# Spreading the weight-narrowing steps of the first chunk and moving one w_out product

## The chip, the cores and the metric

The kernel runs on one core of a Trainium2 chip. The metric is the device time of one execution in microseconds (us); less is better. A core has TensorE (PE, matrix products), VectorE (DVE), ScalarE (ACT), GpSimd (POOL) and SyncE (SP), which here issues all transfers. Each engine takes its own instructions in order, and semaphores make it wait for the others.

## The reference

Three stages follow one another, with a batch of 8, 8 heads, 576 positions of 64 values, and 4608 tokens of 512 values in all:

```python
p_packed = sm_attn(p, k, v)               # 32 packed queries per head
x = sm_attn(q, p_packed, p_packed)        # then tokens x 512
xn = x / rms * rms_g
g = xn @ w_gate; val = xn @ w_val         # 512 x 1536
x = (g * sigmoid(g) * val) @ w_out        # 1536 x 512
h = x @ w_in                              # 512 x 2048
out = (max(h, 0) + alpha * min(h, 0)) @ w_out2
```

The weight matrices come as 64-bit floats, the other inputs and the output are 32-bit floats.

## The kernel before, in words

**Chunks and tiles.** The first two stages run together over 12 chunks of tokens (up to 512 each), the third stage follows. This change touches chunk 0 alone (c = 0), which runs with 512 tokens. A chunk passes through 12 tiles f of 128 of the 1536 hidden values. For each tile TensorE computes the gate group and the value group (`blk_in`, L1012, into the PSUM banks g and v), ScalarE the Silu of g (L1071), VectorE the product s with v (L1078). In odd tiles s is then split into a high part hh on ScalarE and a remainder hl on VectorE, with the remainder in_l of the tile's w_out block in between (both L113); in even tiles of chunk 0 it is used as it is. `blk_out(f)` (L1033) multiplies s by the tile's block of w_out into four banks y: on L1037 for even tiles of chunk 0, on L122 to L124 for odd ones. It is called one tile late, as `blk_out(f - 1)`.

**Narrowing.** The weights come as 64-bit words. `narrow` (L224) makes a unit of 128 x 512 weights into 32-bit floats in two halves. Half A is L227 on VectorE and L231 on ScalarE, half B is L233 on VectorE and then L236 on GpSimd, whose result is the finished unit. There are 36 units: for every pair of tiles j, four units of gate and value weights (gv) and two of w_out (o). `conv_all` (L323) is a generator that takes two units at a time and yields after every half, so a pair is four steps: A, A, B, B. With the end of a unit, which it notices at the step after the pair's last B, it counts the unit in `n_conv` and issues further loads on the SP queue (`loads_to`), as far as load buffers are free (8 for the first 18 units, 4 for the others). A narrowed gv unit is also stored to DRAM for the later chunks; the last three are stored only with unit 34. `conv(n)` runs n steps, `conv_to(n)` runs steps until n units are counted.

**Places in a tile.** `work(f, at)` runs at four places of a tile: 1 after the Silu, 2 after s and its splitting, 3 after the first burst, 4 after the second. It lets the attention chains for the next tokens make their VectorE and ScalarE steps and then, in chunk 0, runs narrowing steps: two at each of the places 1, 2 and 3, none at 4. `burst(f, 2)` and `burst(f, 3)` put TensorE work of these chains (transposes, scores: L420, L429, L442, L481, L600, L617) into the queue.

**Jobs.** The gate and value weights are first multiplied by the packed attention output. `wg_job(b, j)` (L725) does this for batch b and pair of tiles j with 16 matmuls on L735, four for each of its four gv units, and splits the two results (wgh, wgl), which `blk_in` of the tiles 2j and 2j+1 reads. In chunk 0, job (0, 0) runs in the prologue, job (0, j+1) at the start of `burst(f, 2)` of tile f = 2j+1, hence in the tiles 1, 3, 5, 7 and 9, and job (1, 0) in tile 11. Job (0, 5) also issues the reloads of stored units for the jobs (1, 0) and (1, 1) into the ring of 8 gv buffers (L722).

**Order.** The kernel schedules by hand: every engine runs its instructions in the order in which the program issues them. At the start of a tile of chunk 0 the kernel before calls

```python
j1 = (f + 1) // 2
conv_to(min(6 * j1 + (5 if f % 2 else 6), NU1))
```

and the order around the job is

```python
burst(f, 2)            # in chunk 0 with the tile's job ahead
work(f, 3)
if 0 < f < NF - 1:
    blk_out(f - 1)
if f < NF - 1:
    burst(f, 3)
```

In `both` (L359), called at the end of the even tiles of chunk 0, the w_out unit of the next tile is split.

Of the kernel before, what the change touches and what calls it, by code (L numbers as in the profile page):

```python
# [18 lines left out]
def attention_moe_moe2_kernel(ctx, tc, q, k, v, p, w_gate, w_val, w_out, rms_g, w_in2, w_out2, alpha, out):  # L19
# [8 lines left out]
    NF = FF // 128  # L28
# [97 lines left out]
    with tc.manual_schedule():  # L126
# [65 lines left out]
        NU1 = len(units)  # L192
# [24 lines left out]
        def new_gv():  # L217
            return one.tile([128, 4, 128], F32, tag="gv", name="gv_raw", bufs=8)
# [19 lines left out]
        def conv_unit(n):  # L238
            if n == NU1 // 2:
                sg_ctx.close()  # L240
                late_pools["wg2"] = ctx.enter_context(tc.tile_pool(name="wg2", bufs=NWG - NWG1, reuse_waits="tile"))
            u = units[n]
            w = new_gv() if u[0] == "gv" else wa.tile([128, 4, 128], F32, tag="w", name="w_raw")
            yield from narrow(staged.pop(n), w)
            raw[u] = w
            if u[0] == "gv":
                stores.append((u[1], w))
            while stores and (len(stores) > 3 or n >= NU1 - 2):
                i, w = stores.pop(0)
                nc.sync.dma_start(out=gv_dram[i], in_=w.rearrange("p c x -> p (c x)"))  # L250
            yield

        def conv_late():
# [55 lines left out]
                products((5, b22), (3, b21))  # L309
            yield  # L310

        n_load, n_conv, n_job = [0], [0], [0]

        def loads_to(n):
            while n_load[0] < min(n, NU1):
# [28 lines left out]
        def conv(n):  # L344
            for _ in range(n):
                next(convs, None)

        def conv_to(n):
            while n_conv[0] < min(n, NU1):
                next(convs)  # L350

        in_s = {}
# [372 lines left out]
        def wg_job(b, j):  # L725
            if b >= B:
                return
            need_k(b)
            n_job[0] += 1
            ts = [bank("wg") for _ in range(G)]  # L730
            us = [raw.pop(("gv", j * 4 + dc)).rearrange("p c x -> p (c x)") for dc in range(HG)]
            for c_ in range(HG):
                for e in range(2):
                    g, h = c_ // 2, c_ % 2 * 2 + (e ^ c_ // 2)
                    nc.tensor.matmul(  # L735
                        out=ts[g][h * NP:(h + 1) * NP, :],
                        lhsT=ppG[b][e * D:(e + 1) * D, c_, :],
                        rhs=us[c_][e * D:(e + 1) * D, :],
                        start=True, stop=True,
                        tile_position=(e * D, h * NP),  # L740
                    )
            for g in range(G):
                pool = wg1 if n_wg[0] % NWG < NWG1 else late_pools["wg2"]
                n_wg[0] += 1
                h_ = pool.tile([128, 512], F32R, tag="wgh", name="wgh")
                l_ = pool.tile([128, 512], F32R, tag="wgl", name="wgl")
                split_hi(h_, ts[g])
                split_lo(l_, ts[g], h_)
                wgt[b, j, g] = (h_, l_)
            m = b * NJ + j  # L750
            for x in (m + 1, m + 2) if m == NJ - 1 else (m + 2,) if m >= NJ else ():
                gv_load(x)
# [184 lines left out]
        for c, (t0, n, cuts) in enumerate(CH):  # L937
# [9 lines left out]
            def work(f, at):  # L947
                live = [ch for ch in chains["k"] if ch.kind is not None][:1] + chains["q"]
                swap = c > 0 or at == 3 and any(ch.kind == X or ch.kind == M for ch in live)
                if swap and c == 0:  # L950
                    preload(ACTF.Exp)
                for ch in live:
                    n_ = 0
                    while n_ < 2:
                        if ch.kind == R and (at == 1 or at > 2 and (ch is first[0] or n_ == 0)):
                            pass
                        elif n_ == 0 and ch.kind == E and (c == 0 or at < 4) or swap and ch.kind == M:
                            pass
                        elif ch.kind == X and swap and (c == 0 or at == 1 and n_ == 0 or f == NF - 1):
                            pass  # L960
                        else:
                            break
                        ch.last = (c, f, at)
                        ch.next()
                        n_ += 1
                if swap and c == 0:
                    preload(ACTF.Silu)
                if c == 0:
                    conv(2 if at < 4 else 0)

            def q_turn(now, free):
                for n_, ch in enumerate(chains["q"]):
# [21 lines left out]
            def burst(f, at):  # L994
                first[0] = None
                if at == 3 and c and any(ch.kind == X for ch in chains["k"]):
                    return
                jobs = JOBS[c].get(f, ()) if at == 2 else ()
                for jb in jobs if c == 0 else ():
                    wg_job(*jb)  # L1000
                now = [(c, f, x) for x in ((1, 2)[c == 0:] if at == 2 else (2, 3) if c else ())]
                free = 0 if jobs and c else 2
                need = any(ch.b not in ppG for ch in chains["q"])
                if need and (at == 2 or f % 2 == 0):
                    q_turn(now, k_turn(now, free))
                else:
                    k_turn(now, q_turn(now, free))
# [25 lines left out]
            def blk_out(f):  # L1033
                if c == 0 and f % 2 == 0:
                    h, w = hs.pop(f), raw["o", f]
                    for d in range(KD):
                        nc.tensor.matmul(out=ybk[d], lhsT=w[:, d, :], rhs=h, start=f == 0, stop=f == NF - 1)  # L1037
                    return
                oh, ol = in_s.pop(("o", f))
                hh, hl = hs.pop(f)  # L1040
                for d in range(KD):
                    mm3(ybk[d], oh[:, d, :], ol[:, d, :], hh, hl, f == 0, f == NF - 1)

            for f in range(NF):
                if c == 0 and f == 1:
                    held, hold[0] = hold[0], None
                    for i in held:
                        load_q(i)
                if c == NP1 - 2 and f == 9:
                    y_rows.append(load_rows(0, 0))  # L1050
                if c == 6 and f == 6:
                    nc.sync.dma_start(out=alpha_sb, in_=alpha.rearrange("(f p) -> p f", p=128))
                if c == 0:
                    j1 = (f + 1) // 2
                    conv_to(min(6 * j1 + (5 if f % 2 else 6), NU1))
                if last:
                    if f == 0:
                        assert next(late, late) is late
                        prepare = prep(0)
                    if f > 0:  # L1060
                        next(prepare, None)
                    if f in (2, 4, 6, 8, 10):
                        next(prepare, None)
                    if f > 2:
                        load_next()
                tg = blk_in(f, 0, "g")
                s = ring.tile([128, T], F32, tag="s", name="s")[:, 0:n]
                if c:
                    nc.scalar.activation(out=s, in_=tg, func=ACTF.Tanh, scale=0.5)  # L1069
                else:  # L1070
                    nc.scalar.activation(out=s, in_=tg, func=ACTF.Silu)  # L1071
                work(f, 1)
                if c:
                    nc.vector.scalar_tensor_tensor(  # L1074
                        out=s, in0=s, scalar=1.0, in1=tg, op0=ALU.add, op1=ALU.mult
                    )
                tv = blk_in(f, 256, "v")
                nc.vector.tensor_tensor(out=s, in0=s, in1=tv, op=ALU.mult)  # L1078
                for jb in JOBS[c].get(f, ()) if c else ():
                    wg_job(*jb)  # L1080
                exact = c == 0 and f % 2 == 0
                hs[f] = s if exact else hsplit(s, n)
                if c and 0 < f < NF - 2:
                    work(f, 2)
                if not exact:
                    split_lo(hs[f][1], s, hs[f][0])
                if not (c and 0 < f < NF - 2):
                    work(f, 2)
                burst(f, 2)
                work(f, 3)  # L1090
                late_step(c, f, True)
                if 0 < f < NF - 1:
                    blk_out(f - 1)
                if f < NF - 1:
                    burst(f, 3)
                    work(f, 4)
                if f < NF - 1 and (c or f % 2 == 0):
                    both(("o", f + 1))
                late_step(c, f, False)
            tail = [NF - 2, NF - 1]  # L1100
# [309 lines left out]
```

## Time and profile before

| | us |
|---|---|
| median of 3 runs | 1598.16 |
| lowest and highest | 1597.54, 1599.58 |
| the profiled execution | 1597.45 |
| its span in the profile | 1595.7 |

The profile shows one execution. Times in rows are microseconds from the start of the span. A row of the timeline gives start, length, engine, line and operation, the tile written and those read, shapes, the number of instructions merged, and in brackets the idle time before it and what ended it. PE rows are matmuls. Windows give the busy time of the engines in a stretch and the granted TensorE clock (1.00 is full). A chunk's tile is counted here from its first gate matmul: tile 0 starts at 44.54, tile 1 at 50.90, tile 2 at 69.73, tile 3 at 76.61. The first chunk lies in the first 153 us of the span.

### The profile page before, as it was taken

What the parts mean: (1) busy time and instruction counts of PE and PEld (TensorE: products, weight loads), DVE (VectorE), ACT (ScalarE), POOL (GpSimd) and SP (SyncE); (2) the same over time, 40 slices, a digit from 0 to 9 for tenths busy, and PEclk for the clock granted to TensorE, in tenths of its full rate; (3) what the DMA queues carried; (4) which work ended last, traced back from release to release, by engine and by line L of the source; (5) the groups of instructions that cost most, each with busy time, mean ns of one, the idle gap of its engine ahead of it and who ended that gap; (6) DMA issues with size and microseconds to landing.
All of it is one profiled execution on the core that took longest, in us unless ns stands there. A gap on an engine that the chain in (4) does not pass through costs nothing.

```text
span 1595.7 us, 31864 instructions
## 1 busy us (share of the span) xinstructions
PE 1555.4 (97%) x11762; PEld 1364.9 (86%) x11762; DVE 1161.2 (73%) x2232; ACT 887.8 (56%) x1894; POOL 175.7 (11%) x178
## 2 busy tenths in 40 slices
PE   7799999999999999999999999999999999999999
PEld 5457888887878888889889889988998899999998
DVE  6985766666666666766667778777877787788785
ACT  4666555655556554655555556555655555565564
POOL 1541330111201111211120000000000000000000
PEclk8999999999999999999999999999999999999999
DMA  9886777756677566775555676867676767788776
GB/s 267 275 277 200 232 255 223 220 176 224 225 227 252 161 204 213 261 255 169 205 179 180 192 217 184 250 201 217 185 248 201 211 184 250 260 264 291 259 242 198
DMA packets 239067, 356.29 MB, mean 223 GB/s; under 512 B 63424, under 2 KB 97216, under 8 KB 238912
## 3 DMA queue, kind: packets, MB, share of 16 engines
q1 hardware_dynamic: 238912, 354.25, 70.8%
q8 instruction: 94, 1.54, 0.4%
q14 instruction: 61, 0.50, 0.1%
HBM read 296.50 MB, written 57.67 MB: 222 GB/s over the span
## 4 chain that ended last, share of the span: by engine, by line
PE 82%; DVE 8%; ACT 5%; DMA 2%; issue 1%; SPq 1%; POOL 0%; DVEq 0%; ACTq 0%; POOLq 0%
PE ps_g L122 13%; PE ps_g L123 12%; PE ps_g L124 12%; PE ps_y L122 9%; PE ps_y L123 9%; PE ps_y L124 9%; PE ps_wg L735 3%; PE ps_v L122 3%; PE ps_v L123 2%; PE ps_v L124 2%; PE ps_y L1037 1%; DVE hl L113 1%; ACT hh L110 1%; DVE wgl L113 1%; PE ps_at L658 1%
## 5 line engine op out<-in xcount | busy, mean ns | idle before, releaser
L122 PE MATMUL ps_g<-yh,w 128*128 128x512 f32 (+1 forms) x560 | 206.8, 369 | 2.2 <-DVE tmp L1154 2.2
L123 PE MATMUL ps_g<-yl,w 128*128 128x512 f32 (+1 forms) x560 | 206.3, 368 | 0.0
L124 PE MATMUL ps_g<-yh,w 128*128 128x512 f32 (+1 forms) x560 | 205.7, 367 | 0.0
L122 PE MATMUL ps_y<-hh,in_h 128*128 128x320 f32 (+1 forms) x552 | 195.0, 353 | 0.2
L123 PE MATMUL ps_y<-hl,in_h 128*128 128x320 f32 (+1 forms) x552 | 185.4, 336 | 2.5 <-DVE hl L113 2.4
L124 PE MATMUL ps_y<-hh,in_l 128*128 128x320 f32 (+1 forms) x552 | 184.4, 334 | 0.0
L110 ACT ACTIVATE hh<-kept 128x512 fp32r<-128x512 f32 (+1 forms) x200 | 116.5, 587 | 104.7 <-PE ps_g L123 57.6
L124 PE MATMUL ps_y<-w,hl 128*128 128x256 f32 x576 | 163.4, 284 | 1.5 <-DVE hl L113 1.2
L123 PE MATMUL ps_y<-w,hh 128*128 128x256 f32 x576 | 162.8, 283 | 0.0
L122 PE MATMUL ps_y<-w,hh 128*128 128x256 f32 x576 | 162.5, 282 | 0.0
L110 ACT ACTIVATE hh<-s 128x320 fp32r<-128x320 f32 (+1 forms) x138 | 71.9, 521 | 143.6 <-DVE s L1078 143.4
L122 PEld LDWEIGHTS ps_y<-hh,in_h 128*128 128x128 f32 x552 | 103.6, 188 | 47.5 <-issue 39.2
L113 DVE TENSOR_TENSOR hl<-kept,hh 128x512 fp32r<-128x512 f32 (+1 forms) x200 | 123.3, 632 | 16.2 <-ACT hh L110 15.3
L124 PE MATMUL ps_g<-w,hl 128*128 128x256 f32 x432 | 122.3, 283 | 0.0
L123 PE MATMUL ps_g<-w,hh 128*128 128x256 f32 x432 | 122.3, 283 | 0.0
L122 PE MATMUL ps_g<-w,hh 128*128 128x256 f32 x432 | 122.2, 283 | 0.0
L1154 DVE TENSOR_TENSOR tmp<-tmp,ps_g 128x512 f32<-128x512 f32 (+2 forms) x140 | 88.4, 631 | 45.8 <-PE ps_g L124 45.8
L122 PEld LDWEIGHTS ps_g<-yh,w 128*128 128x128 f32 x560 | 105.4, 188 | 15.5 <-DVE tmp L1154 3.7
L122 PE MATMUL ps_g<-xh,wgh 128*128 128x256 f32 (+3 forms) x352 | 114.1, 324 | 2.7 <-ACT qT L602 1.9
L124 PEld LDWEIGHTS ps_g<-yh,w 128*128 128x128 f32 x560 | 105.1, 188 | 13.5
L123 PEld LDWEIGHTS ps_g<-yl,w 128*128 128x128 f32 x560 | 105.5, 188 | 11.3
L1074 DVE SCALAR_TENSOR_TENSOR s<-s,ps_g 128x320 f32<-128x320 f32 (+1 forms) x132 | 70.6, 535 | 59.4 <-ACT s L1069 58.6
(199 smaller groups left out, 4078.5 us busy)
## 6 DMA issues: line engine op xcount, KB each, us to landing
w<-w_dram SPq DMA_DIRECT2D x280, 256.0 KB, 3.0
w<-o_dram SPq DMA_DIRECT2D x280, 256.0 KB, 3.0
gv_raw<-gv_dram SPq DMA_DIRECT2D x168, 256.0 KB, 4.2
in_l<-lo_dram SPq DMA_DIRECT2D x119, 256.0 KB, 4.5
w<-in_moe_w_out_dram SPq DMA_DIRECT2D x28, 512.0 KB, 5.1
w_dram<-w7o SPq DMA_DIRECT2D x56, 256.0 KB, 2.5
o_dram<-w7o SPq DMA_DIRECT2D x56, 256.0 KB, 2.8
vt<-in_v_dram SPq DMA_DIRECT2D x16, 576.0 KB, 6.3
```

The lines of the kernel that those rows point to most:

```text
L110: nc.scalar.activation(out=hi, in_=src, func=ACTF.Copy)
L113: nc.vector.tensor_tensor(out=lo, in0=src, in1=hi.bitcast(F32), op=ALU.subtract)
L122: nc.tensor.matmul(out=o, lhsT=lh, rhs=rh, start=first, stop=False, skip_group_check=more)
L123: nc.tensor.matmul(out=o, lhsT=lh, rhs=rl, start=False, stop=False, skip_group_check=more)
L124: nc.tensor.matmul(out=o, lhsT=ll, rhs=rh, start=False, stop=last, skip_group_check=more)
L658: nc.tensor.matmul(out=t4[r][:, (k_ * G + g) * 128:(k_ * G + g + 1) * 128], lhsT=AT[rows, g, k_ * rw:(k_ + 1) * rw], rhs=ppbd[par][rows, g ...
L735: nc.tensor.matmul(out=ts[g][h * NP:(h + 1) * NP, :], lhsT=ppG[b][e * D:(e + 1) * D, c_, :], rhs=us[c_][e * D:(e + 1) * D, :], start=True, ...
L1037: nc.tensor.matmul(out=ybk[d], lhsT=w[:, d, :], rhs=h, start=f == 0, stop=f == NF - 1)
L1074: nc.vector.scalar_tensor_tensor(out=s, in0=s, scalar=1.0, in1=tg, op0=ALU.add, op1=ALU.mult)
L1154: nc.vector.tensor_tensor(out=out, in0=x, in1=y, op=ALU.add)
```

## The change

Steps are counted as units done right after a unit's second half (`n_done`) and not after its end; `conv_to` goes by this count. `work` runs one step at place 1, two at place 2 and three at place 3. The call at the start of the tile goes; a job calls `conv_to` for the gv units that it reads, and `both` is preceded by one for its w_out unit. In tile 1 of chunk 0, `blk_out(0)` is called before `burst(1, 2)`, so ahead of job (0, 1), and not after `work(1, 3)`.

```diff
@@ conv_unit
                 nc.sync.dma_start(out=gv_dram[i], in_=w.rearrange("p c x -> p (c x)"))
+            n_done[0] += 1
             yield
@@
-        n_load, n_conv, n_job = [0], [0], [0]
+        n_load, n_conv, n_job, n_done = [0], [0], [0], [0]
@@
         def conv_to(n):
-            while n_conv[0] < min(n, NU1):
+            while n_done[0] < min(n, NU1):
                 next(convs)
@@ work
                 if c == 0:
-                    conv(2 if at < 4 else 0)
+                    conv(at % 4)
@@ burst
                 for jb in jobs if c == 0 else ():
+                    conv_to(6 * ((f + 1) // 2) + 4)
                     wg_job(*jb)
@@ for f in range(NF)
-                if c == 0:
-                    j1 = (f + 1) // 2
-                    conv_to(min(6 * j1 + (5 if f % 2 else 6), NU1))
@@
                 if not (c and 0 < f < NF - 2):
                     work(f, 2)
+                ahead = c == 0 and f == 1
+                if ahead:
+                    blk_out(0)
                 burst(f, 2)
                 work(f, 3)
                 late_step(c, f, True)
-                if 0 < f < NF - 1:
+                if 0 < f < NF - 1 and not ahead:
                     blk_out(f - 1)
                 if f < NF - 1:
                     burst(f, 3)
                     work(f, 4)
                 if f < NF - 1 and (c or f % 2 == 0):
+                    if c == 0:
+                        conv_to(6 * (f // 2) + 6)
                     both(("o", f + 1))
```

## Rows read from the trace of the kernel before

**Rows 1.** The page's first part: busy time, share of the span and instructions of each engine
```profile
PE 1555.4 (97%) x11762; PEld 1364.9 (86%) x11762; DVE 1161.2 (73%) x2232; ACT 887.8 (56%) x1894; POOL 175.7 (11%) x178
```

**Rows 2.** Windows, tiles 0 and 1: length, busy us of each engine, TensorE clock, DMA
```profile
44.54:50.90 6.36, 4.26 (x26) 3.50 (x27) 6.36 (x8) 5.11 (x9) 3.93 (x3) 1.00 0.36 94
...
50.90:69.73 18.83, 12.76 (x59) 5.22 (x57) 18.80 (x26) 8.84 (x18) 10.79 (x9) 0.82 1.04 324
```

**Rows 3.** Waits of TensorE, 38 to 160 us: total us, times, longest
```profile
PE ps_at L442 <- DVE s L1078: 4.5, 1, 4.5
...
PE ps_at L429 <- DVE s L1078: 2.1, 1, 2.1
...
PE ps_wg L735 <- POOL gv_raw L236: 1.8, 3, 1.2
```

**Rows 4.** Timeline, tiles 0 to 2: start us, us, engine, line, what it did
```profile
49.84 0.67 DVE L1078 TENSOR_TENSOR s<-s,ps_v 128x512 f32<-128x512 f32 x1
...
53.49 0.39 PE L124 MATMUL ps_v<-xh,wgl 128*128 128x512 f32 x1
...
54.81 2.93 DVE L227 TENSOR_SCALAR w_raw<-w 128x512 int32<-128x512 int32 x2
...
62.31 0.67 DVE L1078 TENSOR_TENSOR s<-s,ps_v 128x512 f32<-128x512 f32 x1
...
73.46 0.42 DVE L227 TENSOR_SCALAR w_raw<-w 128x512 int32<-128x512 int32 x1
```

**Rows 5.** Timeline of TensorE at the end of tile 1
```profile
63.04 1.21 PE L442 MATMUL ps_at<-kT,pT 64*32 64x288 f32 x14 [4.48 <-DVE s L1078]
...
64.18 5.24 PE L1037 MATMUL ps_y<-s,w_raw 128*128 128x512 f32 x8
```

**Rows 6.** Timeline of tile 3, around its job
```profile
79.54 1.09 PE L735 MATMUL ps_wg<-gv_raw,ppG 64*32 64x512 f32 x16
...
79.71 0.69 DVE L1078 TENSOR_TENSOR s<-s,ps_v 128x512 f32<-128x512 f32 x1 [0.85 <-PE ps_v L124]
...
80.92 3.60 PE L1037 MATMUL ps_y<-s,w_raw 128*128 128x512 f32 x8
...
81.10 0.69 DVE L113 TENSOR_TENSOR hl<-s,hh 128x512 fp32r<-128x512 f32 x1
...
81.70 0.68 DVE L233 SCALAR_TENSOR_TENSOR gv_raw<-w,gv_raw 128x512 int32<-128x512 int32 x1
...
82.70 1.30 POOL L236 TENSOR_TENSOR gv_raw<-gv_raw,w 128x512 int32<-128x512 int32 x1 [2.23 <-ACT wgh L110]
```

**Rows 7.** Windows of TensorE: length, busy us, granted clock, DMA share, GB/s
```profile
49.00:50.00 1.00, 0.00 (x0) 1.00 0.96 367
...
60.50:61.00 0.50, 0.00 (x0) 0.50 1.24 237
...
67.00:67.50 0.50, 0.50 (x2) 0.70 1.07 397
```

**Rows 8.** Timeline of ScalarE: the Silu of tile 2
```profile
71.67 0.59 ACT L1071 ACTIVATE s<-ps_g 128x512 f32<-128x512 f32 x1
```

**Rows 9.** Timeline of tiles 5 and 7, at their jobs
```profile
95.07 1.09 PE L735 MATMUL ps_wg<-gv_raw,ppG 64*32 64x512 f32 x16
...
99.07 1.29 POOL L236 TENSOR_TENSOR gv_raw<-gv_raw,w 128x512 int32<-128x512 int32 x1 [2.17 <-DVE gv_raw L233]
...
114.20 0.66 PE L600 MATMUL ps_at<-ident,qt 128*128 128x128 f32 x4 [0.77 <-DVE s L1078]
...
114.69 3.60 PE L1037 MATMUL ps_y<-s,w_raw 128*128 128x512 f32 x8
```

**Rows 10.** Timeline of tile 9, at its job
```profile
128.57 1.09 PE L735 MATMUL ps_wg<-gv_raw,ppG 64*32 64x512 f32 x16
...
130.93 0.70 DVE L647 STREAM_TRANSPOSE A2T<-A 128x512 f32<-128x512 f32 x1
```

**Rows 11.** Waits of the SP queue, 38 to 160 us
```profile
SPq L722 <- PE ps_wg L735: 15.9, 2, 14.3
```

## The prediction

> **What bounds the kernel now.** The page comes first: TensorE is busy in 97% of the span [rows 1], so outside the first 150 us a microsecond is won or lost only where TensorE itself waits. The windows cut along the tiles of the first chunk (a tile starts with the first gate matmul) show the one place where it does: of the 6.36 us of tile 0 it is busy 4.26, of the 18.83 us of tile 1 it is busy 12.76 [rows 2]. That is 2.10 + 6.07 = 8.2 us of idle time. The waits name the reason: 4.5 us and 2.1 us on the VectorE product s (L1078), 1.8 us on GpSimd's last narrowing operation (L236) [rows 3]. The VectorE timeline shows why s is late [rows 4]: in tile 1 TensorE is through with the value matmuls at 53.9, but s starts at 62.31, because the narrowing operations forced at the tile's start stand in front of it. They are slow there: two L227 take 2.93 us where one alone takes 0.42, since GpSimd's L236 runs beside them. After the wait the w_out product of tile 0 takes 5.24 us [rows 5], while the same product takes 3.60 in tile 3 [rows 6]: the granted clock had fallen from 1.00 (2.4 GHz) to 0.50 (1.2 GHz) during the wait, and came back only at 67.2 [rows 7].
>
> **Where the steps go.** I counted the steps by hand. A pair of units is four steps: first half A of both, then second half B of both. The prologue runs 12 steps (units 0 to 5). Before, counting ended units costs one step more in the prologue and six at the start of tile 1; after that six run per tile, so tile f's job finds 6f+23 steps done. After the change nothing is forced anywhere: 1+2+3 is again six per tile, and the job of tile f=2j-1 finds 12j+9 done. It needs 12j+8. The fourth gate unit's B is therefore the first step of place 2, right in front of the job, in each of the tiles 1, 3, 5, 7 and 9; before it was nine steps, a tile and a half, earlier. The narrowing ends in tile 9 instead of tile 8. No instruction is added or removed.
>
> **Gain in tiles 0 to 2.** In tile 0 one L227 instead of two and a B stands before s, so s comes at about 47.9 instead of 49.84 [rows 4], and the 2.1 us wait shrinks to some 0.3. In tile 1 six operations with GpSimd beside them remain before s; at the pace of [rows 4] it comes near 54 instead of 62.31. Tile 0's product now fills 3.60 us before the job. Its cover is not complete: s is still some 2 us behind TensorE, and behind it come in_l, hl, B and L236, so the job's last four matmuls wait about 2.6 us. Then the product no longer covers the softmax that follows: the Exp table load, exponentials and Silu table load lie between L442 and the next Silu. Before, L442 ended at 64.25 and that Silu started at 71.67 [rows 5, 8], 7.4 us. I put that at 6, with fewer narrowing operations in between; TensorE has some 4.3 us of work under it (L442 0.9, transposes 0.4, the next tile's two matmul groups 3.0), so about 1.7 us show. Removed: 8.2 idle, 1.6 for the product at half clock, 0.5 for L442 beside it and some 1 for job matmuls slowed piecemeal, 11.3 in all; still there: 0.3 + 2.6 + 1.7 = 4.6. **Gain 7 us.** Ends: 4, if the job and the Silu each come 1.5 us later still; 10, if all idle time and the slow product go.
>
> **Loss at the jobs of tiles 3, 5, 7 and 9.** Here no product is moved ahead: the job directly follows the value matmuls on TensorE. Before, it starts at 79.54 in tile 3 and ends 1.09 us later, its inputs long ready [rows 6]. The place where the fourth unit's B now stands can be read in the same rows, since another unit's B stands there before: s 79.71, hl 81.10, B 81.70, L236 from 82.70 for 1.30, so 84.00. Twelve of the 16 matmuls need only earlier units; the last four would end at 84.3 instead of 80.6: **3.7 us**. Tile 5 the same way: job at 95.07, L236 from 99.07 to 100.36 [rows 9], end 100.7 instead of 96.2, **4.5**. In tile 7 the wait would again be about 3.6, until 116.1 with the job's end, and 1.1 us of transposes bring the product to 117.2. But TensorE already waited there, 0.77 us for s before the second half of these transposes, and began the product at 114.69 [rows 9]; net **2.5**. In tile 9 a transpose (L647, 0.70 from 130.93) stands in front of the place [rows 10], then B 0.68, a hand-over of 0.3 and L236 1.30: end near 134.2 instead of 129.7, **4.5**. Sum 15.2. What stands behind the job on TensorE is the tile's attention matmuls, the product of tile f-1 and the next tile's gate matmuls, so everything moves. VectorE and ScalarE catch up in the meantime, but TensorE has no idle time left in these tiles that could absorb it. Lower end 13 (3.7 in 3, 5 and 9, 2 in 7), upper end 16.5.
>
> **The clock after these waits.** A wait of 4.5 us was followed by the 0.50 stretch, and the product in it cost 5.24 - 3.60 = 1.6 more; the wait of 2.1 us before 50.57 left the clock at 1.00 [rows 7]. My waits of 3.6 to 4.6 us lie near the longer one, and right behind each comes such a product. I charge three of four (not tile 7's): **5 us**. Ends: 0, and 4 x 2.1 = 8.4 with the slow attention matmuls. The Trainium skill, TensorE: Matmul & The Clock Gate, section "HAM oscillation — how this bites in real kernels", tells of a kernel in which every wait between groups brings the half rate back. By that all four would be charged, and the sum would be 1.6 higher; the 2.1 us wait shows that not every wait does it here.
>
> **Queues.** SP: the loads follow the counted ends, so they are issued seven steps later, but each still comes four steps ahead of its A, as before; cost 0, hidden by the tile in between; 1 us at most in a tile if one lands late, as in tile 7 before. The last three stores of narrowed gate weights now stand behind the reload for job (1,1), which finds their buffers still taken and must wait for job (1,0) in tile 11. Nothing else of SP's is queued in that stretch: before, its next issue was waiting 14.3 us for that same job [rows 11]. Job (1,1) comes only in the next chunk: 0, and 3 at most if the reload lands late.
>
> **Sum.** -7 + 15.2 + 5 = +13. The profiled execution took 1597.45 us (span 1595.7), 0.7 under the median 1598.16 and just under the fastest run, 1597.54; against the median I say 1611.
>
> **Rivals.**
> (1) *Faster: the jobs find their inputs.* If TensorE did not stand still at the four jobs, only the gain remains: 1598.2 - 7 = 1591. This decides as soon as the four waits together cost under 7 us, 1.8 each. For it: before, TensorE shows no wait at these four jobs, and three of the job's four units still come early. Against it: s, in_l, hl, B and L236 follow one another through semaphores, and [rows 6] give 4.5 us from the job's start to the end of L236. TensorE's queue could also take the product of tile f-1, which is ready, in front of the waiting job. Against that: in tile 1 the product of tile 0 was ready from 50.5 on, and TensorE stood still until 63.04 behind the waiting L442 [rows 4, 5]. The Trainium skill, same page, opening table, gives this queue a partial reorder window. Its section on the steps of a matmul limits that to weight loads and keeps matmuls in order, which the trace bears out. 0.11.
> (2) *Balance.* Gain 10, waits of 2.5 us each and no clock loss: 1598. Waits that short would need B ahead of hl. 0.05.
> (3) *Waits without a clock loss.* 1598.2 + 8 = 1606. For it: the clock's fall depends on where a wait lies, and there are only a few samples. 0.27, inside the range.
> (4) *Late reload.* The SP queue held until tile 11 also delays chunk 1: 3 us more, 1614. 0.07.
> My forecast, waits plus clock: 0.50.
>
> **The numbers.** Slower: 0.50 + 0.27 + 0.07 = 0.84; same 0.05; faster 0.11; 0.2% (3 us) is about what a measurement of this kernel can tell from no change. Range: from -10 + 13 + 0 = +3 (1601) to -4 + 16.5 + 8.4 = +21 (1619); rivals 1 and 2 stay outside.
>
> **What would show it.** Right: in tile 1 s starts within 3 us of the last value matmul; TensorE waits about 3.6 to 4.6 us for L236 at L735 in tiles 3, 5 and 9; clock 0.50 stretches lie around those products; tile 2 starts 7 to 9 us earlier; the first chunk ends some 13 us later. Wrong: job waits of under 1.8 us, or a chunk 0 that ends before 150.

## The result and the profile after

The changed kernel takes **1618.64 us** (median of 4 runs, 1615.77 to 1619.52); the kernel before, run beside it, 1597.85. The ratio is 1.0128, 95% interval 1.0110 to 1.0146: slower by 21 us. The profiled execution took 1618.42 us, its span is 1616.6.

The page's first part for the changed kernel answers to [rows 1]:

```profile
PE 1567.2 (97%) x11762; PEld 1367.7 (85%) x11762; DVE 1159.4 (72%) x2232; ACT 888.2 (55%) x1894; POOL 176.4 (11%) x178
```

The counts are those of before; TensorE is busy 11.8 us longer and idle 9.1 us more. All of it lies in the first chunk, which ended at 152.44 us before and ends at 173.39 now: 20.95 us of the 20.9 by which the spans differ. The lengths of its tiles (from one first gate matmul to the next) say where. The windows of TensorE, tiles 0 and 1, then 3, 5, 7 and 9 (length, busy us of PE, PEld, DVE, ACT and POOL, clock, DMA share, GB/s):

```profile
44.65:48.97 4.32, 4.23 (x26) 3.50 (x27) 4.32 (x6) 3.88 (x7) 2.91 (x2) 1.00 0.41 140
48.97:61.29 12.32, 9.60 (x60) 4.72 (x58) 10.01 (x14) 5.84 (x11) 5.87 (x5) 1.00 1.00 284
...
69.52:83.90 14.38, 11.82 (x59) 5.19 (x56) 8.88 (x13) 5.26 (x10) 7.31 (x6) 0.88 0.76 251
91.26:109.26 18.00, 14.76 (x101) 6.84 (x95) 9.52 (x24) 8.05 (x15) 6.96 (x5) 0.81 0.60 187
115.59:129.97 14.38, 11.09 (x62) 5.06 (x61) 9.60 (x16) 6.51 (x11) 6.40 (x5) 1.00 0.83 266
136.82:156.11 19.29, 13.99 (x71) 6.06 (x69) 12.78 (x22) 10.10 (x20) 7.22 (x6) 0.82 0.60 181
```

Tiles 0 and 1 took 6.36 and 18.83 before [rows 2]; the four odd tiles took 8.12, 10.05, 10.31 and 9.40. So tiles 0 and 1 give 8.5 us, tile 2 takes 1.35 back (8.23 for 6.88), and the four tiles lose 6.3, 7.95, 4.1 and 9.9: 28.2. The other tiles stay within 0.2 us. The waits of TensorE up to 175 us answer to [rows 3]:

```profile
PE ps_wg L736 <- POOL gv_raw L236: 16.7, 10, 2.8
```

The waits for s (4.5 and 2.1 us) are gone, and ten waits for GpSimd at the job stand in their place, where there were three of 1.8 us in all [rows 3]. The timeline of tile 1 shows the gain (rows 4 and 5 of before):

```profile
51.81 3.59 PE L1039 MATMUL ps_y<-s,w_raw 128*128 128x512 f32 x8
...
54.04 0.67 DVE L1077 TENSOR_TENSOR s<-s,ps_v 128x512 f32<-128x512 f32 x1
...
55.33 1.31 PE L736 MATMUL ps_wg<-gv_raw,ppG 64*32 64x512 f32 x12
...
58.82 0.62 PE L736 MATMUL ps_wg<-gv_raw,ppG 64*32 64x512 f32 x2 [2.18 <-POOL gv_raw L236]
```

s starts at 54.04 and not at 62.31, and the product takes 3.59 us and not 5.24. The timeline of tile 3 shows the loss [rows 6]:

```profile
72.44 1.06 PE L736 MATMUL ps_wg<-gv_raw,ppG 64*32 64x512 f32 x8
72.51 1.29 POOL L236 TENSOR_TENSOR gv_raw<-gv_raw,w 128x512 int32<-128x512 int32 x1 [1.10 <-PE ps_v L124]
72.61 0.69 DVE L1077 TENSOR_TENSOR s<-s,ps_v 128x512 f32<-128x512 f32 x1 [0.32 <-PE ps_v L124]
73.22 1.13 DVE L113 TENSOR_TENSOR in_l<-w_raw,in_h 128x512 fp32r<-128x512 f32 x1
...
73.86 1.05 PE L736 MATMUL ps_wg<-gv_raw,ppG 64*32 64x512 f32 x4 [0.36 <-POOL gv_raw L236]
74.28 0.68 DVE L113 TENSOR_TENSOR hl<-s,hh 128x512 fp32r<-128x512 f32 x1
74.88 0.68 DVE L233 SCALAR_TENSOR_TENSOR gv_raw<-w,gv_raw 128x512 int32<-128x512 int32 x1
...
75.78 1.28 POOL L236 TENSOR_TENSOR gv_raw<-gv_raw,w 128x512 int32<-128x512 int32 x1 [1.97 <-DVE gv_raw L233]
...
77.11 1.30 PE L736 MATMUL ps_wg<-gv_raw,ppG 64*32 64x512 f32 x4 [2.20 <-POOL gv_raw L236]
...
79.00 4.69 PE L1039 MATMUL ps_y<-s,w_raw 128*128 128x512 f32 x8
```

Behind s stand in_l, hl, the fourth unit's half B (L233) and its L236, one after the other as the prediction had it: L236 ends 4.6 us after the job's start. The job, 1.09 us before, now lasts from 72.44 to 78.41: three pieces of 1.06, 1.05 and 1.30 us with two waits between. The product behind it takes 4.69 us. The windows around it (columns as above) show the clock falling behind the second wait, which ended at 77.11. In tile 7, after a wait of the same 2.20 us that ended at 123.94, it did not:

```profile
76.00:77.00 1.00, 0.00 (x0) 0.00 (x0) 0.49 (x1) 0.00 (x0) 1.00 (x1) 1.00 1.01 223
77.00:78.00 1.00, 0.89 (x4) 0.14 (x4) 0.00 (x0) 0.00 (x0) 0.06 (x1) 0.89 1.06 388
78.00:79.00 1.00, 1.00 (x5) 0.65 (x4) 0.00 (x0) 0.56 (x1) 0.00 (x0) 0.50 1.03 396
...
124.00:125.00 1.00, 1.00 (x5) 0.16 (x6) 0.00 (x0) 0.00 (x0) 0.00 (x0) 1.00 0.36 129
```

### The profile page after: what moved, and what is told of

The parts are those of the page before. It is cut to its first block, busy times and chain, and to the rows that moved or that the text cites. A ratio compares the mean times of both kernels' runs of the same rounds, so it can differ in the third digit from the quotient of the medians.

```text
span 1616.6 us, 31851 instructions
## 1 busy us (share of the span) xinstructions
PE 1567.2 (97%) x11762; PEld 1367.7 (85%) x11762; DVE 1159.4 (72%) x2232; ACT 888.2 (55%) x1894; POOL 176.4 (11%) x178
## 4 chain that ended last, share of the span: by engine, by line
PE 78%; DVE 6%; ACT 4%; DMA 1%; issue 1%; POOL 0%; SPq 0%; DVEq 0%; ACTq 0%
PE ps_g L122 13%; PE ps_g L123 12%; PE ps_g L124 12%; PE ps_y L122 9%; PE ps_y L123 8%; PE ps_y L124 8%; PE ps_wg L736 3%; PE ps_v L122 2%; PE ps_v L123 2%; PE ps_v L124 2%; DVE hl L113 1%; ACT hh L110 1%; PE ps_at L659 1%; DVE yl L113 1%; PE ps_g L1029 1%
## 5 line engine op out<-in xcount | busy, mean ns | idle before, releaser
L122 PEld LDWEIGHTS ps_g<-yh,w 128*128 128x128 f32 x560 | 105.4, 188 | 15.4 <-DVE tmp L1158 3.7
L124 PEld LDWEIGHTS ps_g<-yh,w 128*128 128x128 f32 x560 | 105.1, 188 | 13.6
L123 PEld LDWEIGHTS ps_g<-yl,w 128*128 128x128 f32 x560 | 105.5, 188 | 11.3
```

The costliest lines, as they stand in the source:

```text
L122: nc.tensor.matmul(out=o, lhsT=lh, rhs=rh, start=first, stop=False, skip_group_check=more)
L123: nc.tensor.matmul(out=o, lhsT=lh, rhs=rl, start=False, stop=False, skip_group_check=more)
L124: nc.tensor.matmul(out=o, lhsT=ll, rhs=rh, start=False, stop=last, skip_group_check=more)
```

## The experiments

The theory at the start: the loss is the lateness of the last half B, and what the clock adds after it; the gain comes from the steps that no longer stand in front of s. "Lead" is the number of steps that a job finds done beyond those it needs; by the count of the prediction it was 9 before and is 1 after. All numbers of the runs stand in one table: median, ratio to the kernel before on the same chip with its 95% interval, and tile lengths of the profiled execution, each worked out as above. Tile 0 started between 44.5 and 46.6 us in these executions, so tile lengths tell more than single spans.

| run | lead | median us | ratio | tiles 0-2 | 3 | 5 | 7 | 9 | others |
|---|---|---|---|---|---|---|---|---|---|
| before | 9 | 1597.85 | 1 | 32.1 | 8.1 | 10.0 | 10.3 | 9.4 | 37.9 |
| after | 1 | 1618.64 | 1.0128 (1.0110 to 1.0146) | 24.9 | 14.4 | 18.0 | 14.4 | 19.3 | 37.8 |
| e1 | 2 | 1607.92 | 1.0057 (1.0042 to 1.0072) | 23.8 | 11.3 | 15.6 | 12.6 | 15.2 | 37.9 |
| e2 | 9 | 1597.73 | 0.9992 (0.9983 to 1.0001) | 31.4 | 8.1 | 10.0 | 10.2 | 9.5 | 38.0 |
| e3 | 1 | 1605.30 | 1.0041 (1.0027 to 1.0056) | 25.8 | 9.7 | 12.5 | 12.0 | 15.2 | 39.5 |
| e4 | 1 | 1614.12 | 1.0095 (1.0077 to 1.0113) | 24.9 | 12.7 | 15.4 | 14.9 | 16.5 | 37.8 |
| e5 | 1 | 1622.91 | 1.0151 (1.0134 to 1.0168) | 29.1 | 14.1 | 17.1 | 17.0 | 18.2 | 37.8 |
| e6 | 4 | 1599.14 | 1.0004 (0.9995 to 1.0014) | 23.8 | 11.0 | 11.1 | 12.3 | 10.8 | 39.8 |
| e7 | 7 | 1600.60 | 1.0014 (1.0003 to 1.0024) | 25.9 | 12.2 | 12.5 | 11.8 | 11.4 | 37.9 |
| e8 | 8 | 1605.51 | 1.0042 (1.0027 to 1.0057) | 32.8 | 8.1 | 11.7 | 13.7 | 10.3 | 38.7 |
| e9 | 5 | 1598.10 | 1.0000 (0.9991 to 1.0008) | 23.7 | 11.0 | 11.1 | 10.0 | 13.6 | 38.4 |
| e10 | 3 | 1597.81 | 0.9997 (0.9988 to 1.0006) | 23.8 | 11.0 | 11.6 | 11.0 | 11.8 | 37.9 |
| e11 | 9 | 1599.65 | 1.0008 (0.9999 to 1.0017) | 26.2 | 12.7 | 10.0 | 10.0 | 9.4 | 39.6 |
| e12 | 3 | 1595.57 | 0.9980 (0.9971 to 0.9989) | 23.8 | 9.1 | 10.8 | 11.2 | 12.4 | 37.8 |

**e1, one step more of lead**: the changed kernel with two, two, two.

```diff
-                    conv(at % 4)
+                    conv(2 if at < 4 else 0)
```

> The changed kernel with the spread put back to two, two, two (nothing forced, w_out product of tile 0 still moved ahead in tile 1). The job of a tile then has the half B of its fourth gate unit at place 1, one step before s, and not right in front of it. Theory (the loss is the lateness of that last half B, by one step of the spread): the job's waits for GpSimd in tiles 3, 5, 7 and 9 fall from 2.2 to 2.8 us to under 1 us each, no stretch at clock 0.50 follows them, the gain of 7 us in tile 1 mostly stays (one more step before s takes up to 1.5 us of it): 1592 to 1599. Rival (the forced steps of the kernel before were what kept the jobs supplied, and without them the jobs stay late whatever the spread): waits of over 1.5 us stay in at least three of the four tiles, 1608 to 1618.

The direction was right, the size was not: half the loss comes back, which puts the time at the lower edge of the rival's range, and the clock still falls in tiles 5 and 9 (mean 0.89 in each). The job's waits in its timeline, tile 3:

```profile
73.03 3.23 POOL L236 TENSOR_TENSOR gv_raw<-gv_raw,w 128x512 int32<-128x512 int32 x2 [1.11 <-ACT s L1070]
...
74.61 1.05 PE L736 MATMUL ps_wg<-gv_raw,ppG 64*32 64x512 f32 x4 [0.47 <-POOL gv_raw L236]
...
76.32 1.05 PE L736 MATMUL ps_wg<-gv_raw,ppG 64*32 64x512 f32 x4 [0.66 <-POOL gv_raw L236]
```

Both half Bs now stand ahead of s, but their two L236 need 3.23 us on GpSimd, and the job still runs in three pieces.

**e2, the move alone**: the kernel before with `blk_out(0)` ahead of `burst(1, 2)`.

```diff
+                ahead = c == 0 and f == 1
+                if ahead:
+                    blk_out(0)
                 burst(f, 2)
...
-                if 0 < f < NF - 1:
+                if 0 < f < NF - 1 and not ahead:
```

> The kernel before with the moved w_out product alone (steps forced at the start of a tile and two, two, two as before). Theory (the gain of 7 us in tile 1 comes from the six steps that no longer stand in front of s; the move only fills a wait once s is early): s of tile 1 still starts near 62, the product runs ahead of the job at its own 3.6 us only if the clock is up, and the span falls by 0.5 to 2 us: 1596 to 1597.5. Rival (the move is the gain): 1591 to 1594.

As the theory had it, s of tile 1 starts at 62.71 and the time hardly moves (0.2 us above the theory's range): by 1.1 us, and the interval of the ratio includes no change. While s is late the move is worth little.

**e3, the product ahead in every odd tile.**

```diff
-                ahead = c == 0 and f == 1
+                ahead = c == 0 and f in (1, 3, 5, 7, 9)
                 if ahead:
-                    blk_out(0)
+                    blk_out(f - 1)
```

> The changed kernel with the w_out product of the tile before moved ahead of the job in tiles 3, 5, 7 and 9 too, not in tile 1 alone. The spread stays one, two, three, so the half B comes as late as in the changed kernel. Theory (TensorE stands still at the job only because nothing ready is queued ahead of it): the product's 3.6 us covers the third and fourth unit's waits, which fall to under 1 us in tiles 3, 5 and 7 (in tile 9, where they are 5.3 us in all, some 1.5 us stay), the clock stays at 1.00; of the 28 us lost in these tiles 18 to 24 come back: 1594 to 1601. Rival (the late job also delays what follows on the other engines: the split of wgh and wgl and the next tile's gate matmuls, so the wait only moves there): the waits go to the next tile's first gate or value matmuls, 1606 to 1615.

The four tiles give back 16.6 of their 28.2 us, tile 10 takes 1.7 of it (8.13 for 6.44). The time falls between the two ranges, nearer the rival's: more than half of the loss is TensorE standing at the job with ready work behind it, but the job remains late, single waits of 1.4, 1.2 and 2.8 us stay in tiles 5, 7 and 9, and in tile 9 the clock still falls (mean 0.90).

**e4, the wait filled with work**: the third unit's matmuls are done three times, which writes the same values again.

```diff
-            for c_ in range(HG):
+            order = (0, 1, 2, 2, 2, 3) if b == 0 and j > 1 else range(HG)
+            for c_ in order:
```

> The changed kernel with the job matmuls of the third gate unit repeated twice more in tiles 3, 5, 7 and 9, ahead of those of the fourth unit: 2.1 us of additional TensorE work that writes the same values again, in a time in which TensorE waited 2.2 to 2.8 us for the fourth unit. Nothing is supplied earlier. Theory (part of the loss is the half clock that follows the standstill): the clock stays at 1.00 through the products of tiles 3, 5 and 9, which take 3.6 us and not 4.7 to 5.1, and the tiles get 4 to 7 us shorter in sum: 1612 to 1615. Rival (the clock falls for another reason, or the slow products only fill time that another wait would take): 1618 to 1620, with the products as slow as before.

The timeline of tile 3 (L737 and L1040 are the job and the product here):

```profile
75.89 2.77 PE L737 MATMUL ps_wg<-gv_raw,ppG 64*32 64x512 f32 x12 [0.34 <-POOL gv_raw L236]
79.15 1.05 PE L737 MATMUL ps_wg<-gv_raw,ppG 64*32 64x512 f32 x4 [0.49 <-POOL gv_raw L236]
...
80.50 3.60 PE L1040 MATMUL ps_y<-s,w_raw 128*128 128x512 f32 x8
```

The last piece starts 7.6 us into tile 3 in both kernels (8.3 in tile 5, 10.3 in tile 9), so nothing is supplied earlier; but the product takes 3.60 us for 4.69, and the windows of tiles 3, 5 and 9 (columns as above) show the clock at 1.00:

```profile
71.56:84.30 12.74, 11.90 (x67) 4.93 (x64) 8.87 (x13) 5.14 (x10) 6.12 (x6) 1.00 0.86 288
91.65:107.02 15.37, 13.84 (x109) 6.28 (x102) 9.55 (x24) 7.84 (x15) 6.96 (x5) 1.00 0.70 219
...
135.06:151.59 16.53, 12.94 (x79) 5.74 (x78) 12.79 (x22) 9.66 (x20) 5.94 (x5) 1.00 0.67 212
```

Tiles 3, 5 and 9 get shorter by 1.6, 2.6 and 2.8 us; tile 7, whose clock had stayed up, gets 0.5 longer, since the repeated matmuls push its last piece back by 0.5. The price of the clock is thus 7.0 us by tiles. More work made the kernel faster.

**e5, without the move.**

```diff
-                ahead = c == 0 and f == 1
+                ahead = False
```

> The changed kernel without the moved product (in tile 1 the w_out product of tile 0 stands behind the job again). The spread and the late half B stay. Theory (in tile 1 s is early, so TensorE has 2 to 4 us of job waits and nothing to fill them but the product): tile 1 gets 3 to 5 us longer than the 12.3 us of the changed kernel, all else stays: 1620 to 1624. Rival (the move does nothing, as it did almost nothing in the kernel before): 1617 to 1620.

Within the theory: tile 1 takes 17.88 us for 12.32, its clock 0.81, and tile 2 gives 1.3 back. With s early the move is worth 4.3 us; with s late (e2) it was worth 1, not clear of the noise.

**e6 to e8, the lead and the spread.** e6 puts two steps more into tile 2, e7 puts six into tiles 1 and 2 under the changed spread, e8 is the kernel before with the changed spread alone.

```diff
-                    conv(at % 4)
+                    conv(2 if at < 4 or f == 2 else 0)
```

> The changed kernel with two, two, two and two more steps at place 4 of tile 2, so that every later job finds 4 steps more than it needs, where two, two, two alone gave it 2 and the changed kernel 1. Theory (the loss is a lack of lead: with 2 steps the two last L236 of a job still follow one another on GpSimd during the job, 3.2 us in tile 3, while with 4 steps both lie in the tile before): job waits under 0.5 us in tiles 3, 5, 7 and 9, whose lengths come back to within 0.7 us each of those of the kernel before (8.1, 10.1, 10.3, 9.4); with the gain of tiles 0 to 2 less 1 to 3 us for the two steps more: 1589 to 1595. Rival (spreading the narrowing over tiles 3 to 9 and a tile longer costs VectorE and GpSimd time there whatever the lead): the four tiles stay 3 us or more longer in sum, 1596 to 1602.

```diff
-                    conv(at % 4)
+                    conv(3 if at == 4 and f in (1, 2) else at % 4)
```

> The changed kernel with the lead alone put back: spread one, two, three and the moved product stay, and three more steps run at place 4 of tile 1 and three at place 4 of tile 2, so that a job finds 7 steps more than it needs, where the kernel before gave it 9. Theory (lack of lead is the whole loss, the spread itself none): waits at the jobs of tiles 3, 5, 7 and 9 under 0.5 us, those tiles within 0.7 us each of the kernel before; the six steps take 1 to 4 us of the gain of 8.4 us that tile 2's later Silu showed: 1590 to 1596. Rival (one, two, three itself costs, three steps at place 3 delaying the softmax or the next Silu): the waits go, but the span stays above that of the kernel before, 1600 to 1606.

```diff
-                    conv(2 if at < 4 else 0)
+                    conv(at % 4)
```

> The kernel before (steps forced at a tile's start, product not moved) with the spread one, two, three alone. Theory (six steps per tile and the lead of nine stay, only the places change): s comes one operation earlier in tile 0, and later tiles change by under 0.5 us each: 1595 to 1599. Rival (one, two, three itself costs): 1600 to 1606.

e6 and e7 bring the time down by 19.5 and 18 us, to within 0.2% of the kernel before. In e7 nothing but the lead differs from the changed kernel, so the lack of lead is most of the loss. But neither gets below the kernel before, and all three times (e6, e7 and e8) lie in the ranges of the rivals. In e6 tiles 3, 5, 7 and 9 stay 7.4 us longer in sum, and the gain of 8.3 us in tiles 0 to 2 is gone again by tile 10. And e8 says that one, two, three costs 6.6 us by its median even with a lead of 8, most of it in tiles 5 and 7 (1.6 and 3.4). Part of that is the clock again: in tile 7 the job's second half starts after a wait of 2.17 us, and the tile's mean clock is 0.88. I had held the spread for free. In e7, behind the moved product, it shows less: its median is 1 to 3 us above those of e6 and of e9 to e11, which run two, two, two with leads of 3 to 9.

**e9 to e11, how the steps meet.** A new theory for what stays: with an even number of steps two half Bs share a place, their L236 run in a row, and L227 pairs beside them take 2.9 us. e9, e10 and e11 put three, one and seven steps more into the kernel with two, two, two.

```diff
-                    conv(at % 4)
+                    conv(2 if at < 4 else 3 if f == 2 else 0)
```

> The changed kernel with two, two, two and three more steps at place 4 of tile 2: one step more than in the run with two, so that a place holds a half A and a half B and no longer two of the same half. Theory (what was left of the loss is the pairing: two half Bs in one place send two L236 in a row to GpSimd, 3.0 to 3.2 us, and the two L227 beside them take 2.9 us where two alone take 0.9, so s and the job come late): the L227 pairs of 2.6 to 2.9 us vanish from tiles 3, 5, 7 and 9, those tiles are within 0.7 us each of the kernel before, tiles 0 to 2 keep 7 us: 1590 to 1594. Rival (only the amount of lead counts, and one step more adds little): 1596 to 1599, as with two.

```diff
-                    conv(at % 4)
+                    conv(2 if at < 4 else 1 if f == 2 else 0)
```

> The changed kernel with two, two, two and a single step more at place 4 of tile 2: one step fewer than in the run with two, again with a half A and a half B in each place. Theory (pairing): in spite of less lead than the run with two it is no slower than that by more than the wait for the fourth unit, whose half B is now the first step of place 1: 1.5 to 2 us in each of four tiles, with one job piece of 1.05 us; the L227 pairs vanish: 1595 to 1601, against 1608 with two, two, two alone. Rival (lead alone counts): midway between 1608 and 1599, 1602 to 1605.

```diff
-                    conv(at % 4)
+                    conv(2 if at < 4 else {1: 4, 2: 3}.get(f, 0))
```

> The changed kernel with two, two, two and seven more steps, four at place 4 of tile 1 and three at place 4 of tile 2: from tile 3 on it has done as many steps as the kernel before, in the same places. Theory: tiles 3 to 9 take the kernel before's 8.1, 7.4, 10.1, 6.4, 10.3, 6.8 and 9.4 us to 0.3 each; the gain of tiles 0 to 2 shrinks by what seven steps cost behind the second product in tile 1 and in tile 2, 2 to 5 us of 8: 1592 to 1596. Rival (the move of the steps behind the job and the Silu only shifts the wait, to tile 2's s or its attention matmuls): no gain left, 1597 to 1600.

The pairing theory missed in e9: the time is in the rival's range, there is no gain, and the pair is still there in tile 3 (L227 twice in 2.93 us at 73.51), probably because the engines run behind the order in which the steps are issued. e10 came out as pairing had it, but equally says that a lead of 3 is enough: 2 gave 1607.9, 3 to 5 give 1597.8 to 1599.1. Between e1 and e10 both the lead and the pairing change, so what pairing costs stays open. e11, in its rival's range too, shows where the gain goes. From tile 5 on its tiles are those of the kernel before, but tiles 2 to 4 take 31.8 us and not 22.4. Its windows of tiles 1 to 3 (columns as above):

```profile
50.22:60.53 10.31, 9.45 (x59) 4.59 (x57) 10.31 (x14) 5.35 (x9) 6.41 (x4) 1.00 0.95 271
60.53:70.63 10.10, 7.66 (x39) 5.82 (x40) 10.06 (x13) 8.64 (x19) 5.96 (x4) 0.99 1.07 296
70.63:83.32 12.69, 10.00 (x57) 5.49 (x55) 12.66 (x18) 5.83 (x11) 8.00 (x6) 0.87 1.00 321
```

The third busy figure is VectorE's: 10.31, 10.06 and 12.66 us of 10.31, 10.10 and 12.69. It has no time left there, as it had none in tile 1 before (18.80 of 18.83, [rows 2]). Steps taken out of tile 1 and put back a tile or two later cost 9.4 us in tiles 2 to 4, where tiles 0 and 1 had given 9.1.

**e12, the version from these runs**: two, two, two, one step more in tile 1, and the product ahead in tiles 1, 3, 5 and 7.

```diff
-                    conv(at % 4)
+                    conv(2 if at < 4 else 1 if f == 1 else 0)
...
-                ahead = c == 0 and f == 1
+                ahead = c == 0 and f in (1, 3, 5, 7)
                 if ahead:
-                    blk_out(0)
+                    blk_out(f - 1)
```

> The changed kernel with two, two, two, one step more at place 4 of tile 1 (in the run with a lead of one it stood in tile 2), and the w_out product of the tile before ahead of the job in tiles 1, 3, 5 and 7. Theory (what keeps the gain of 8 us of tiles 0 to 2 from showing is lead, pairing and a standing job): in tile 3 no two L236 follow one another ahead of the job (they did after the step in tile 2, 2.95 us), and the product covers what is left of the waits; tiles 3, 5 and 7 come within 0.6 us each of the kernel before, tile 9 stays 2.4 us longer, tiles 0 to 2 take 23.8 to 25 us against 32.1: 1591 to 1595. Rival (the narrowing taken out of tiles 0 and 1 is VectorE and GpSimd time that costs as much wherever it stands): 1596 to 1599.

It is faster than the kernel before by 2.8 us, 0.1 to 0.3%. The time lies between the ranges of the theory and of the rival, so it settles neither. Its tile 3:

```profile
71.12 2.96 POOL L236 TENSOR_TENSOR gv_raw<-gv_raw,w 128x512 int32<-128x512 int32 x2 [1.11 <-DMA w<-in_moe_w_gate_dram]
71.13 3.59 PE L1039 MATMUL ps_y<-s,w_raw 128*128 128x512 f32 x8
...
74.66 1.09 PE L736 MATMUL ps_wg<-gv_raw,ppG 64*32 64x512 f32 x16
```

The two L236 still follow one another, against what I expected, but the product covers them, and the job runs its 16 matmuls in one piece of 1.09 us. Tiles 3, 5 and 7 are 1.0, 0.7 and 0.9 us longer than before, tile 9, without the product ahead, 3.0.

## Why the prediction was right, and where it was off

The sign and the mechanism were right; 1611 was 8 us too low. That the result lies inside the range, 0.4 us below its top, is luck: the loss at the jobs was 21.1 us, outside its own range of 13 to 16.5, and only the unused ends of the other two terms (a gain of 4, a clock of 8.4) made room for it.

- **Where the steps go.** Right. Before the job stand s, in_l, hl, B and L236; the last L236 ends 4.6 us after the job's start in tile 3 (forecast 4.46) and 5.3 in tile 5 (98.26 + 1.28 - 94.24; forecast 5.3). The sign that the prediction named, waits of 3.6 to 4.6 us, was not there in that form: the third unit's piece splits them, and the last waits are 2.20, 2.48 and 2.80 in tiles 3, 5 and 9.
- **Gain of 7 in tiles 0 to 2.** Right: 7.2 (32.1 to 24.9). s at 54.04 (forecast 54), the last wait 2.18 (2.6), tile 2 longer by 1.35 (1.7). e2 and e5 show that it needs the early s, and that the move adds 4.3 to it.
- **Loss of 15.2 at the jobs.** This is the term that was mis-sized. Without the clock (tiles 3, 5 and 9 of e4, whose clock stayed up, and tile 7 of the changed kernel, against those of before) it is 4.6, 5.3, 4.1 and 7.1: 21.1 where I had 3.7, 4.5, 2.5 and 4.5. First, I let the last four matmuls take 0.3 us, a quarter of the 1.09 of all 16; alone they take 1.05, so 0.75 more in each tile: 3.0 of the 5.9 us, and nearly all that is missing in tiles 3 and 5. Second, the third unit is late too: TensorE waits 0.36, 0.76, 1.09 and 2.50 us for it, and its own piece takes 1.05 again. That adds nothing by itself, since the fourth unit comes later still, but in tiles 7 and 9 its L236 runs beside in_l, which takes 1.50 and 1.53 us (0.70 in the rows of tile 3 that I went by). Third, tile 9, the kernel before first:

```profile
128.94 0.69 DVE L1078 TENSOR_TENSOR s<-s,ps_v 128x512 f32<-128x512 f32 x1 [0.50 <-ACT s L1071]
129.54 0.69 DVE L113 TENSOR_TENSOR in_l<-w_raw,in_h 128x512 fp32r<-128x512 f32 x1
```

  and the changed kernel:

```profile
135.88 2.99 DVE L227 TENSOR_SCALAR gv_raw<-w 128x512 int32<-128x512 int32 x2
...
140.46 0.69 DVE L643 TENSOR_TENSOR A<-A,s 128x512 f32<-128x512 f32 x1
...
141.06 0.68 DVE L233 SCALAR_TENSOR_TENSOR gv_raw<-w,gv_raw 128x512 int32<-128x512 int32 x1
141.67 0.68 DVE L1077 TENSOR_TENSOR s<-s,ps_v 128x512 f32<-128x512 f32 x1
...
142.26 1.53 DVE L113 TENSOR_TENSOR in_l<-w_raw,in_h 128x512 fp32r<-128x512 f32 x1
...
143.30 1.05 PE L736 MATMUL ps_wg<-gv_raw,ppG 64*32 64x512 f32 x4 [2.50 <-POOL gv_raw L236]
...
147.15 1.06 PE L736 MATMUL ps_wg<-gv_raw,ppG 64*32 64x512 f32 x2 [2.80 <-POOL gv_raw L236]
147.16 1.22 PE L443 MATMUL ps_at<-kT,pT 64*32 64x288 f32 x12
148.01 1.06 PE L736 MATMUL ps_wg<-gv_raw,ppG 64*32 64x512 f32 x2
```

  Before, s came 3.3 us into tile 9 (128.94 - 125.65), and I left it there. It now comes at 4.85: the attention chain in front of it (up to L643) is late, since two L227 (2.99 us from 135.88) run into the tile, and the third unit's B stands between, where the kernel before had no narrowing left.
- **Clock, 5.** The price was 7.0. The product alone costs 1.1, 1.2 and 1.4 us (forecast 1.6 each); the rest is that the slow stretch takes in the job's last piece and the transposes too (L736 1.30 us in tile 3). The tiles were right (3, 5 and 9, not 7), but by luck. The term rested on waits near the 4.5 us that had lowered the clock, and single waits of 2.20 to 2.80 lowered it. Nothing in the prediction sets tile 7 apart either: in e5, after the same two waits, its clock falls and the last piece takes 1.92 us. Tile 7 of the changed kernel, then of e5:

```profile
120.68 1.05 PE L736 MATMUL ps_wg<-gv_raw,ppG 64*32 64x512 f32 x4 [1.09 <-POOL gv_raw L236]
...
123.94 1.05 PE L736 MATMUL ps_wg<-gv_raw,ppG 64*32 64x512 f32 x4 [2.20 <-POOL gv_raw L236]
```

```profile
123.66 1.05 PE L736 MATMUL ps_wg<-gv_raw,ppG 64*32 64x512 f32 x4 [1.09 <-POOL gv_raw L236]
...
126.91 1.92 PE L736 MATMUL ps_wg<-gv_raw,ppG 64*32 64x512 f32 x4 [2.20 <-POOL gv_raw L236]
```

- **Queues, 0.** Right: job (1, 1) runs at 180.21 without a wait, in 1.09 us. The next job of chunk 1 does wait 0.85 us (until 193.70), for a reason that was not sought, but by the end the spans differ by no more than the ends of chunk 0 do, 20.9 us.
- **Spread one, two, three.** I costed it by its lead alone. In e8 it costs 6.6 us with a lead of 8, in e7 less; how much of the 21 us is due to it cannot be told from these runs, since it also sets the lead.

Of the rivals, the jobs did not find their inputs (1). Single waits were about as short as (2) had them, 2.20 to 2.80 us, but the jobs cost more than their waits and the clock fell. The clock did fall (3), and the reload cost nothing (4). Under (1) the prediction says that the trace bears out that matmuls keep their order. For the product that holds; but in tile 9 twelve small matmuls of the attention chain (L443, from 147.16), which the program issues behind the job, start before the job's last two (148.01).

## What to carry to other kernels

When work is taken out of the way of one stage, count for each later consumer how many steps of lead it keeps: here leads of 3 to 5 gave the time of the kernel before, 2 took some 10 us more (the pairing of the half Bs changed with it), and 1, with the changed spread, 20. Ready work placed ahead of a consumer that may be late (e3, e12) covers what lead does not. And where the helper engine has no time left, as VectorE in the first tiles, moving its work a few tiles on can move the loss with it: in e11 tiles 2 to 4 lost what tiles 0 and 1 had gained.

## What the runs showed of the hardware

- The cost of a group of matmuls does not divide by its count. 16 job matmuls of 64 x 32 x 512 take 1.09 us, 8 take 1.06, 4 take 1.05: they run side by side. The Trainium skill, TensorEngine Tiling (Array Packing), section "Overview", says that the array can work as several independent smaller ones; the rows agree, and add that arriving one by one loses that.
- The length of a wait alone does not tell whether the clock falls. In the changed kernel waits of 1.09 and 2.20 us left it at 1.00 in tile 7, and the same two waits in the same tile of e5 did not; in tile 5 of e1 it fell at the second of two waits of 1.25 and 0.65 us with a piece of 1.05 between, as its windows show (columns as above). What decides was not settled.

```profile
95.00:96.00 1.00, 0.35 (x4) 0.15 (x4) 1.00 (x1) 0.89 (x2) 0.79 (x1) 0.90 1.04 309
96.00:97.00 1.00, 1.00 (x4) 0.03 (x2) 1.00 (x4) 0.26 (x1) 0.00 (x0) 0.50 1.05 400
```

- L227 on VectorE takes 0.42 us alone [rows 4]; two of them beside two L236 take 3.00, as the changed kernel's timeline at the end of tile 2 shows:

```profile
68.18 3.23 POOL L236 TENSOR_TENSOR gv_raw<-gv_raw,w 128x512 int32<-128x512 int32 x2 [1.32 <-DMA w<-in_moe_w_gate_dram]
...
68.70 3.00 DVE L227 TENSOR_SCALAR gv_raw<-w 128x512 int32<-128x512 int32 x2
```

  The Trainium skill, SBUF — State Buffer, section "SBUF: two separate sides", calls the port pair that VectorE and GpSimd share an exclusive lock, which some VectorE operations must wait for until a whole GpSimd instruction is done; the rows agree: VectorE ends at 71.70, 0.3 us behind GpSimd.
